# A gated Fourier and feed-forward mix on one core: five more couples of its big products at a second Strassen level

## The chip, the cores and the metric

The kernel runs on one core of a Trainium2 chip. The metric is the device time of one execution in microseconds (us); lower is better. TensorE (PE) multiplies, with PEld loading its weights; VectorE (DVE), ScalarE (ACT) and GpSimd (POOL) work on tiles; SyncE (SP) issues most loads.

## The reference, cut to what matters

```python
x = A_x                                            # 2048 x 1024
g = sigmoid((x * gate_w).sum(-1, keepdims=True))
a_ = einsum("bsd,ed->bse", x, dft_hid_re)          # 1024 x 1024 matrices
b_ = einsum("bsd,ed->bse", x, dft_hid_im)
a = einsum("ts,bse->bte", dft_seq_re, a_) - einsum("ts,bse->bte", dft_seq_im, b_)   # 2048 x 2048 matrices
h = relu(x @ w1 + b1) ** 2                         # w1: 1024 x 3584
b = h @ w2 + b2                                    # w2: 3584 x 1024
out = g * a + (1 - g) * b
```

All is float32.

## The kernel before, in words

**Stages.** The work is a list of *steps* in five stages, made in this order: `x_stage` (x times the hidden-dimension matrices, result `ab`), `c_stage` (the sequence stage: `ab` with the 2048 x 2048 matrices, result times g, stored as `gy`), `h_stage(0)` and `h_stage(1)` (the hidden layer, result `h`), and `o_stage` (the output stage: `w2` with `h`, plus bias, times 1 - g, plus `gy`, to `out`). Results between the stages go through DRAM. The list has 425 steps.

**A step** (`Group.run`, L297 to L315) multiplies a stationary operand of up to four column tiles (`rows`) and two contraction tiles with a moving operand of 512 columns. Each float32 operand is split in two: `hi` (a rounded copy, ScalarE, L220) and `lo` (the remainder, VectorE, L230); an operand of half width keeps both in one tile, `both`. Three matmuls (hi hi, hi lo, lo hi, L306) take the place of one, so that a step of four rows is 4 x 2 x 3 = 24 matmuls, one of two rows 12. Sums land in PSUM; the accumulator has four pairs of banks.

**Strassen, first level.** Every stage's product is cut in 2 x 2 blocks and computed as seven products instead of eight (Winograd's form, `seven`, L366), in the order 1, 2, 5, 6, 3, 7, 4. Their factors are blocks or sums of blocks: `SUMS_L` (S1 to S4) and `SUMS_R` (T1 to T4), which VectorE makes at L172 from tiles loaded by SP (L152). Results are put together as products end: `one` and `u` hold partial blocks, c11, c12, c21, c22 the final ones.

**Second level.** In the tall stages (`tall`, L412, for the sequence and the output stage) the contraction has 8 and 7 steps of two tiles (`ksteps`). A product goes either through `direct` (L445; its ksteps x 2 column blocks as steps of 24 matmuls) or through `twice` (L459). `twice` takes the first 2k contraction steps of a product as k *couples*, and computes each couple by seven smaller products of 12 matmuls each; the contraction steps that are left (`rest`) are done plainly. How many couples a product has stands in `TWICE_C` and `TWICE_O` (L20), product number to k. Before, the sequence stage has {2: 4, 3: 3, 4: 2} and the output stage {2: 3, 3: 3}.

The small products 1, 6, 7 and 5 of all couples come first; VectorE puts their results together (`one`, `six`, `seven_`, `five`, L477 to L527; adds at L438, L491, L493, L516, L519) with the partial result `old` that the product adds to, if there is one. Then 2, 4 and 3 are computed onto the blocks so made: `Group.prepare` (L279) has ScalarE copy a block back into PSUM (L293, `ps<-...`). The plain `rest` goes onto the same blocks, as steps of 12 matmuls.

**What sets the order.** One loop (L909 to L966) walks through the steps and puts down every instruction in program order, which each engine follows. For each step it loads tiles up to 12 steps ahead (`LOADS`) as SBUF has room (55 slots of 512 KB), issues POOL's stores, lets finished blocks go through `final` a few steps late (`LATER`), prepares the next step's PSUM, and puts sums, `hi` and `lo` ahead of their use: those due within three (`SUMS`) or two (`RESTS`) steps in any case, others up to nine steps ahead (`SPREAD`) if its own clocks for PE and VectorE say there is time. VectorE's queue thus holds sums, remainders and the putting together of results, in one fixed order.

In the first-level product 6 (L456) the T4 sums that product 4's couples need (`early`) are made while T2 is at hand, and stored to DRAM for product 4; the other T4 sums are made in product 4 from a stored T2.

**The end.** The last product's last block is finished row by row: `last` (L813 to L825) has VectorE add bias, multiply and add `gy` for one row of 512 columns at a time, and stores each at once (SP and ACT queues). Other blocks of `out` go through `final` (L827) and a store by POOL (L936).

Of the kernel before, what the change touches and what calls it, by code (L numbers as in the profile page):

```python
# [16 lines left out]
NF = F // P  # L17
SLOTS, KEEP, RAWS = 55, 5, 4
WIDE, TALL_C, TALL_O = ((1, 2, 5, 6, 3, 7, 4),) * 3
TWICE_X, TWICE_C, TWICE_O = (1, 2, 5, 3, 4), {2: 4, 3: 3, 4: 2}, {2: 3, 3: 3}  # L20
LATER = 3
WARM = 44
FAR_TALL, FAR_WIDE = ("T2",), ()
TWICE_H = (1, 2, 5, 3, 4), (2, 5, 3, 4)
# [17 lines left out]
def gated_mix_kernel(ctx: ExitStack, tc: tile.TileContext, x4, xn, w4, ct, w1a, w1b, w2, b1, b2, gw, out):  # L42
# [276 lines left out]
    def step(st, mv, group):  # L319
        st.uses += 1  # L320
        mv.uses += 1
        steps.append((st, mv, group, []))
        needs = 0
        count[group] = count.get(group, 0) + 1
        if count[group] % group.k == 0:
            needs += group.done[count[group] // group.k - 1][1]
        wanted.append(needs)
# [81 lines left out]
                    ends[e] = len(steps)  # L409
        return ends  # L410

    def tall(left, right, ksteps, order, second, target, final, last=None):  # L412

# [3 lines left out]
        left = {q: Sums(lambda i, j, q=q: left_(i, j, q), SUMS_L, far=FAR_TALL) for left_ in (left,) for q in range(ksteps)}  # L419
# [38 lines left out]

        def twice(p, old, new, ends, drop, sign):  # L459

            l, r = FACTORS[p]
            k = second[p]
            rest = range(2 * k, ksteps)
            more = len(rest)
            tmp = {key: Near("u") for key in ((0, 0),)}

# [67 lines left out]
            for q in range(k):  # L534
                for p2 in (1, 6, 7, 5):
                    l_, r_ = FACTORS[p2]
                    step(l2[q].operand(l_, 256), r2[q].operand(r_), groups[p2])

            def to(m, c):
                key = block(m, c)  # L540
                if last and p == order[-1] and (m, c) == (1, 1):
                    return Group(2, more, (lambda _, ps, row: last(new[key], ps, row), 0, [new[key]]),
                                 onto=[new[key]], by_row=True)
                return Group(2, k * ((m, c) != (1, 1)) + more, (lambda _, ps: put(new, key, ps, ends), 0, [new[key]]),
                             onto=[new[key]])

            groups = {2: to(0, 0), 3: to(0, 1), 4: to(1, 0), None: to(1, 1)}
            for q in range(k):
                again = Sums(lambda j, c, q=q: right[2 * q + j, c].of(r), SUMS_R, True)
                again.made.update({key: r2[q].of(key) for key in ("T1", "T2")})  # L550
                for p2 in (2, 4, 3):
                    l_, r_ = FACTORS[p2]
                    step(l2[q].operand(l_, 256), again.operand(r_), groups[p2])
            own = []
            for q in rest:
                st = left[q].operand(l)
# [223 lines left out]
    def c_stage():  # L780
        rows = [Row(n, False) for n in range(2)]
        to = {}

        def target(i, n, k):
            near = Near("y")
            to[near] = i, n, *k
            return near

        def final(dst, ps):
            i, n, c, rp = to[dst]  # L790
            nc.vector.tensor_tensor(dst.slot, dst.slot if ps is None else ps, rows[n].of(c).broadcast_to([P, 2, 512]),
                                    op=ALU.mult)
            vec(VEC[0] + VEC[1])
            rows[n].used()
            stores.append((gy[i, n, c, rp], dst, 0, 2))

        at = len(steps)
        tall(lambda i, j, q: ab[j, q, i], lambda j, n, q, c: ct[n, c, j, q], 8, TALL_C, TWICE_C, target, final)
        return at, rows


    def o_stage():
# [37 lines left out]

        fetched = {}
        at = len(steps)
        ends = tall(lambda i, j, q: w2[i, j, q], lambda j, n, q, c: h_far[j, q, 2 * n + c], 7, TALL_O, TWICE_O, target, final, last)
        return at, rows, fetched, ends

    def want(k, *items):
# [157 lines left out]
```

## Time and profile before

| | |
|---|---|
| median of 3 runs | 1891.29 us (1889.42 to 1892.37) |
| the profiled execution's own time | 1888.96 us |
| its span, first to last instruction | 1886.9 us |
| mean granted TensorE clock | 0.999 |
| instructions in the span | 21962 |
| ScalarE busy | 1001.3 us (53%) |
| GpSimd busy | 86.8 us (5%) |

A row of the groups or of the timeline names the line, the engine, the operation, the tiles (out<-in) and their shape, then a count, busy time and mean duration; in the timeline the first two numbers are start and length in us, and the brackets give idle time of the engine before it and what ended it. A matmul's record lasts longer than the distance to the next, since matmuls are pipelined. "Waits" rows give who waited for whom: us in total, how often, the longest.

### The profile page before, as it was taken

What the parts mean: (1) busy time and instruction counts of PE and PEld (TensorE: products, weight loads), DVE (VectorE), ACT (ScalarE), POOL (GpSimd) and SP (SyncE); (2) the same over time, 40 slices, a digit from 0 to 9 for tenths busy, and PEclk for the clock granted to TensorE, in tenths of its full rate; (3) what the DMA queues carried; (4) which work ended last, traced back from release to release, by engine and by line L of the source; (5) the groups of instructions that cost most, each with busy time, mean ns of one, the idle gap of its engine ahead of it and who ended that gap; (6) DMA issues with size and microseconds to landing.
All of it is one profiled execution on the core that took longest, in us unless ns stands there. A gap on an engine that the chain in (4) does not pass through costs nothing.

```text
span 1886.9 us, 21962 instructions
## 1 busy us (share of the span) xinstructions
PE 1876.6 (99%) x8288; PEld 1551.3 (82%) x8288; DVE 1610.3 (85%) x1543; ACT 1001.3 (53%) x1123; POOL 86.8 (5%) x161
## 2 busy tenths in 40 slices
PE   9999999999999999999999999999999999999998
PEld 7888888888888888888888888888888888888887
DVE  8997898599777998798896997989976997789882
ACT  6474564363343554455484797767954434264440
POOL 0000110000010000000000000000100001000000
PEclk9999999999999999999999999999999999999999
DMA  5732989339786489383551865628872887629971
GB/s 223 247 121 86 348 288 412 129 117 375 261 312 256 151 322 383 139 312 112 170 198 56 325 228 195 228 84 299 293 259 97 317 336 265 218 103 370 409 300 45
DMA packets 128425, 442.93 MB, mean 235 GB/s; under 512 B 14128, under 2 KB 23616, under 8 KB 128320
## 3 DMA queue, kind: packets, MB, share of 16 engines
q1 hardware_dynamic: 106416, 363.26, 53.0%
q0 software_dynamic: 21472, 77.61, 10.3%
q8 instruction: 65, 1.06, 0.2%
q10 hardware_dynamic: 432, 0.66, 0.1%
q14 instruction: 40, 0.33, 0.1%
HBM read 362.83 MB, written 78.65 MB: 234 GB/s over the span
## 4 chain that ended last, share of the span: by engine, by line
PE 97%; DVE 2%; ACT 0%; DMA 0%; issue 0%; SPq 0%; DVEq 0%; ACTq 0%
PE ps L306 97%; DVE lo L230 1%; DVE h L603 0%; DVE sum L172 0%; DMA raw<-in_w 0%; DVE o L818 0%; ACT u L596 0%; ACT hi L220 0%; DVE o L820 0%; DVE raw L172 0%; SPq L152 0%; DVEq L172 0%; DVEq L230 0%; ACTq L596 0%
## 5 line engine op out<-in xcount | busy, mean ns | idle before, releaser
L306 PE MATMUL ps<-hi 128*128 128x512 f32 x2328 | 905.7, 390 | 4.0 <-ACT hi L220 3.6
L306 PE MATMUL ps<-lo,hi 128*128 128x512 f32 x2328 | 905.3, 389 | 0.0
L306 PE MATMUL ps<-hi,lo 128*128 128x512 f32 x2328 | 904.2, 389 | 0.1
L220 ACT ACTIVATE hi<-raw 128x1024 fp32r<-128x1024 f32 (+2 forms) x413 | 420.6, 1037 | 399.0 <-DVE raw L172 274.1
L230 DVE TENSOR_TENSOR lo<-raw,hi 128x1024 fp32r<-128x1024 f32 (+2 forms) x413 | 484.5, 1199 | 57.5 <-ACT hi L220 31.3
L306 PEld LDWEIGHTS ps<-hi 128*128 128x128 f32 x2328 | 437.2, 188 | 95.9 <-ACT hi L220 4.2
L306 PEld LDWEIGHTS ps<-hi,lo 128*128 128x128 f32 x2328 | 437.1, 188 | 92.0 <-DVE lo L230 1.0
L306 PEld LDWEIGHTS ps<-lo,hi 128*128 128x128 f32 x2328 | 437.3, 188 | 91.0 <-DVE lo L230 0.4
L172 DVE TENSOR_TENSOR raw<-raw 128x1024 f32<-128x1024 f32 (+1 forms) x276 | 326.4, 1207 | 56.4 <-DMA raw<-in_ct 19.4
L220 ACT ACTIVATE hi<-sum 128x1024 fp32r<-128x1024 f32 (+1 forms) x172 | 176.1, 1036 | 184.8 <-DVE sum L172 151.2
L306 PE MATMUL ps<-hi,both 128*128 128x512 f32 x840 | 259.8, 389 | 0.0
L230 DVE TENSOR_TENSOR lo<-sum,hi 128x1024 fp32r<-128x1024 f32 (+1 forms) x172 | 203.3, 1198 | 32.9 <-PE ps L306 16.6
L306 PEld LDWEIGHTS ps<-hi,both 128*128 128x128 f32 x840 | 157.7, 188 | 33.8 <-ACT ps L293 0.7
L306 PE MATMUL ps<-lo,both 128*128 128x512 f32 x420 | 163.5, 389 | 0.0
L172 DVE TENSOR_TENSOR sum<-raw 128x1024 f32<-128x1024 f32 (+1 forms) x116 | 121.9, 1066 | 35.4 <-PE ps L306 28.1
L172 DVE TENSOR_TENSOR sum<-raw,sum 128x1024 f32<-128x1024 f32 (+2 forms) x87 | 96.8, 1119 | 12.0 <-PE ps L306 11.7
L603 DVE TENSOR_TENSOR h<-h,ps 128x1024 f32<-128x1024 f32 x92 | 98.2, 1086 | 9.6 <-ACT u L596 7.1
L596 ACT ACTIVATE u<-ps 128x1024 f32<-128x1024 f32 x76 | 71.9, 950 | 62.0 <-PE ps L306 54.3
L306 PEld LDWEIGHTS ps<-lo,both 128*128 128x128 f32 x420 | 78.8, 188 | 16.1
L293 ACT ACTIVATE ps<-u 128x1024 f32<-128x1024 f32 (+1 forms) x74 | 70.0, 953 | 22.2 <-DVE o L831 12.0
L700 ACT ACTIVATE h<-h,b1c 128x512 f32<-128x512 f32 x112 | 74.3, 712 | 6.3 <-DVE h L603 6.0
L220 ACT ACTIVATE both<-sum 128x512 fp32r<-128x512 f32 x60 | 37.1, 625 | 52.7 <-DVE sum L172 33.4
(61 smaller groups left out, 650.5 us busy)
## 6 DMA issues: line engine op xcount, KB each, us to landing
raw<-in_ct SPq DMA_DIRECT2D x151, 512.0 KB, 6.2
raw<-h SPq DMA_DIRECT2D x132, 512.0 KB, 7.3
raw<-in_x SPq DMA_DIRECT2D x107, 512.0 KB, 5.3
raw<-in_w SPq DMA_DIRECT2D x98, 512.0 KB, 6.3
raw<-ab SPq DMA_DIRECT2D x72, 512.0 KB, 6.8
h<-h POOLq DMA_DIRECT2D x48, 512.0 KB, 5.7
raw<-in_w1a SPq DMA_DIRECT2D x36, 512.0 KB, 5.0
ab<-ab POOLq DMA_DIRECT2D x32, 512.0 KB, 6.7
```

Of the source, the lines that this page charges most:

```text
L172: nc.vector.tensor_tensor(self.slot[:, k, c], src[0][:, k, c], src[1][:, k, c], op=self.op)
L220: nc.scalar.activation(self.hi[:, k, c], self.block.slot[:, k, c], AF.Copy)
L230: nc.vector.tensor_tensor(self.lo[:, k, c], self.block.slot[:, k, c], self.hi[:, k, c].bitcast(F32), op=SUB)
L293: nc.scalar.activation(t[:, :n, :], b.slot[:, at:at + n, :], AF.Copy, scale=self.sign)
L306: nc.tensor.matmul(self.ps[r // self.per][:, r % self.per, :], a[:, kk, r * P:(r + 1) * P], b[:, kk, :], start=self.at == 1 and kk + n == ...
L596: nc.scalar.activation(view(near.slot, k), view(ps, k), AF.Copy, scale=float(sign))
L603: nc.vector.tensor_tensor(view(near.slot, k), view((src or dst)[k].slot, k), view(ps, k), op=ADD if sign > 0 else SUB)
L700: nc.scalar.activation(dst.slot[:, k, :], (dst.slot if ps is None else ps)[:, k, :], AF.Relu, bias=b1c[:, tile0 + k:tile0 + k + 1])
```

## The change

`TWICE_C` gets three couples instead of two for product 4 of the sequence stage; `TWICE_O` gets two couples each for products 1 and 4 of the output stage. New are the lists `FIRST_C` and `FIRST_O`: for a product that has no partial result to add to, or that stands in the list (product 2 of the sequence stage, where nothing is left over; products 2 and 4 of the output stage), the `rest` comes first, as steps of 24 matmuls, onto the old partial result, and leaves its own partial blocks by `put`; the couples then go onto those. In the last product, where no `rest` is left at the end, the small product 4 comes last, and its block is the one that is finished row by row. With four contraction steps of product 4 in couples, the output stage also makes eight of its T4 sums early, in product 6.

```diff
-TWICE_X, TWICE_C, TWICE_O = (1, 2, 5, 3, 4), {2: 4, 3: 3, 4: 2}, {2: 3, 3: 3}
+TWICE_X, TWICE_C, TWICE_O = (1, 2, 5, 3, 4), {2: 4, 3: 3, 4: 3}, {1: 2, 2: 3, 3: 3, 4: 2}
+FIRST_C, FIRST_O = (2,), (2, 4)
...
         def twice(p, old, new, ends, drop, sign):
             l, r = FACTORS[p]
             k = second[p]
             rest = range(2 * k, ksteps)
+            if rest and (not old or p in first):
+                some = [Group(4, len(rest), (lambda rp, ps, c=c: put(new, (c, rp), ps, sign=sign), 2 * (old is not new),
+                                             [new[c, rp] for rp in range(2)]),
+                              onto=old and [old[c, rp] for rp in range(2)], spend=drop) for c in range(2)]
+                sts = {q: left[q].operand(l) for q in rest}
+                for q in rest:
+                    for c in range(2):
+                        step(sts[q], right[q, c].operand(r), some[c])
+                old, rest, drop = new, (), False
             more = len(rest)
...
-                if last and p == order[-1] and (m, c) == (1, 1):
-                    return Group(2, more, (lambda _, ps, row: last(new[key], ps, row), 0, [new[key]]),
+                if last and p == order[-1] and (m, c) == ((1, 1) if more else (1, 0)):
+                    return Group(2, more or k, (lambda _, ps, row: last(new[key], ps, row), 0, [new[key]]),
                                  onto=[new[key]], by_row=True)
...
+            own = []
             for q in range(k):
...
                 for p2 in (2, 4, 3):
                     l_, r_ = FACTORS[p2]
-                    step(l2[q].operand(l_, 256), again.operand(r_), groups[p2])
+                    own.append((l2[q].operand(l_, 256), again.operand(r_), groups[p2]))
+            if last and p == order[-1] and not more:
+                own.sort(key=lambda e: e[2] is groups[4])
+            for e in own:
+                step(*e)
...
-        tall(lambda i, j, q: ab[j, q, i], lambda j, n, q, c: ct[n, c, j, q], 8, TALL_C, TWICE_C, target, final)
+        tall(lambda i, j, q: ab[j, q, i], lambda j, n, q, c: ct[n, c, j, q], 8, TALL_C, TWICE_C, FIRST_C, target, final)
...
-        ends = tall(lambda i, j, q: w2[i, j, q], lambda j, n, q, c: h_far[j, q, 2 * n + c], 7, TALL_O, TWICE_O, target, final, last)
+        ends = tall(lambda i, j, q: w2[i, j, q], lambda j, n, q, c: h_far[j, q, 2 * n + c], 7, TALL_O, TWICE_O, FIRST_O, target, final, last)
```

The list of steps grows from 425 to 434.

More of the change, by code (lines that the diff above doesn't have):

```diff
@@ L410, in seven, with tall @@
         return ends
[L412 removed]
+    def tall(left, right, ksteps, order, second, first, target, final, last=None):
         left = {q: Sums(lambda i, j, q=q: left_(i, j, q), SUMS_L, far=FAR_TALL) for left_ in (left,) for q in range(ksteps)}
```

## The prediction

> **What bounds the kernel now.** I read the page first (span, engines, the chain that ended last), then the chain in order of time, then a table of windows by product of the output stage.
>
> ```profile
> span 1886.9 us, 21962 instructions
> PE 1876.6 (99%) x8288; PEld 1551.3 (82%) x8288; DVE 1610.3 (85%) x1543; ACT 1001.3 (53%) x1123; POOL 86.8 (5%) x161
> PE 97%; DVE 2%; ACT 0%; DMA 0%; issue 0%; SPq 0%; DVEq 0%; ACTq 0%
> ...
> 14.91 1257.50 PE ps L306 x5538
> ...
> 1300.11 577.56 PE ps L306 x2546
> ```
>
> The first two rows say that TensorE matmuls fill 99% of the span; the chain says the same by a stronger measure, 97% of what ended last is matmuls at L306. The two long pieces are unbroken matmul streams: 1257.50 us / 5538 = 0.227 us and 577.56 / 2546 = 0.227 us for each matmul. So the time is the number of matmuls times 0.227 us plus a short head and tail, as long as operands come in time. Whether they do is VectorE's matter (85% busy), and here the average hides the stages. The columns below are PE, PEld, DVE, ACT and POOL busy us; the seven stretches are products 1, 2, 5, 6, 3, 7, 4 of the output stage.
>
> ```profile
> 1364.60:1440.80 76.20, 76.20 (x338) 63.08 (x337) 49.27 (x51) 35.01 (x43) 2.15 (x4) 1.00 0.58 211
> 1440.80:1508.80 68.00, 68.00 (x301) 56.20 (x300) 63.85 (x67) 34.72 (x40) 0.98 (x2) 1.00 0.66 247
> 1508.80:1585.00 76.20, 76.20 (x338) 63.07 (x337) 62.70 (x56) 31.86 (x31) 5.13 (x9) 1.00 0.79 293
> 1585.00:1661.20 76.20, 76.20 (x338) 63.10 (x337) 56.02 (x54) 26.19 (x30) 4.23 (x8) 1.00 0.61 217
> 1661.20:1729.20 68.00, 68.00 (x301) 56.16 (x300) 66.85 (x72) 38.99 (x45) 1.08 (x2) 1.00 0.65 244
> 1729.20:1805.40 76.20, 76.20 (x338) 63.08 (x337) 64.38 (x59) 33.52 (x33) 1.81 (x3) 1.00 0.94 364
> 1805.40:1881.70 76.30, 76.30 (x337) 62.81 (x335) 44.00 (x45) 16.76 (x18) 4.28 (x6) 1.00 0.44 168
> ```
>
> Products 1 and 4 are plain and use VectorE for 49.27 and 44.00 of some 76 us; products 2 and 3, already at the second level, use it for 63.85 and 66.85 of 68.00, with TensorE still full. The change spends the room in the first and the last row.
>
> **TensorE: what is removed.** A couple (two contraction tiles) done plainly takes 4 steps of 24 matmuls, at the second level 7 steps of 12: 84 for 96. Product 4 of the sequence stage goes from two couples to three, products 1 and 4 of the output stage from none to two each: five couples, 60 matmuls. The built programs agree: 8244 matmuls at L306 before, 8184 after; so that the change doesn't do what it says is out. 60 x 0.227 = **-13.6 us**, all on the path, 2.7 in the sequence stage and 5.45 in each of the two products.
>
> The Trainium skill, page "TensorE: Matmul & The Clock Gate", section "Back-to-back issue gap", gives about 131 ns for a sustained matmul of 512 columns. By that the removal would be worth 7.9 us (an estimate); the chain's 0.227 us speaks against it here, so the sum stays with the rows.
>
> **VectorE: what is added.** Pitches, from instructions that stand back to back:
>
> ```profile
> 1435.54 1.23 DVE L230 TENSOR_TENSOR lo<-sum,hi 128x1024 fp32r<-128x1024 f32 x1 [1.43 <-PE ps L306]
> 1436.68 1.22 DVE L230 TENSOR_TENSOR lo<-raw,hi 128x1024 fp32r<-128x1024 f32 x1
> ...
> 1448.91 0.69 DVE L172 TENSOR_TENSOR sum<-raw 128x512 f32<-128x512 f32 x1 [0.31 <-PE ps L306]
> 1449.52 0.68 DVE L230 TENSOR_TENSOR both<-sum,both 128x512 fp32r<-128x512 f32 x1
> ```
>
> The 1024-wide instruction lasts 1.23 us, but the next begins 1436.68 - 1435.54 = 1.14 us after it; the 512-wide one takes 0.61. Each couple adds 4 half-wide left sums, 4 full right sums, 7 half-wide remainders ("both") and, 7 full ones for 6, one full remainder: 11 x 0.61 + 5 x 1.14 = 12.4 us, 62 us for five. Products 1 and 4 of the output stage also put their four partial blocks together (one copy, then 1 + 2 + 2 + 3 adds) in place of plain copies: 8 x 1.14 = 9.1 us each. Together about **80 us of VectorE**: 34 in each of the two output products and 12 in the sequence stage, of which 4 sums (4.6 us) move forward into product 6. The engine's share goes from 1610 / 1887 to some 1690 / 1877 = 90%. ScalarE gets 61 instructions more at 53% busy, and SP one load more; neither was a bound.
>
> **Is it hidden? The margin, counted down VectorE's queue.** The tight place is the start of the output stage, where product 1 used to build the lead that product 2 eats.
>
> ```profile
> 1358.72 2.36 DVE L230 TENSOR_TENSOR lo<-raw,hi 128x1024 fp32r<-128x1024 f32 x2
> ...
> 1387.14 0.70 DVE L230 TENSOR_TENSOR both<-raw,both 128x512 fp32r<-128x512 f32 x1
> ...
> 1440.78 0.39 PE L306 MATMUL ps<-hi,both 128*128 128x512 f32 x1
> ...
> 1493.52 2.35 DVE L230 TENSOR_TENSOR lo<-raw,hi 128x1024 fp32r<-128x1024 f32 x2
> ...
> 1508.84 0.39 PE L306 MATMUL ps<-hi 128*128 128x512 f32 x1
> ```
>
> The first remainder of the stage is done at 1361.1 (1358.72 + 2.36) and its step starts at 1364.6, where the first window begins: a lead of 3.5 us. The first remainder for product 2 is done at 1387.8, 52.9 us before its step at 1440.78. The first of product 5 is done at 1495.9 (it is the second of the pair, 1493.52 + 2.35), 13 us before its step at 1508.84. In the queue of the built program, from the first of these to the last, stand 72 full and 35 half instructions before, 72 x 1.14 + 35 x 0.61 = 103 us, done in 134.8: 31 us were waits, taken out of a lead that could afford them. After, the same stretch holds 91 full and 61 half ones, 141 us, against PE's 144.2 - 5.4 = 138.8 us and the 3.5 us of lead. Without any wait the lead at product 5 is 138.8 + 3.5 - 141 = about 1 us. So this stage has hardly anything over, and every wait that VectorE keeps comes off 1 us. What it waited for:
>
> ```profile
> DVE sum L172 <- PE ps L306: 14.7, 6, 3.9
> DVE g L767 <- DMA g<-g_far: 6.3, 1, 6.3
> ...
> DVE raw L172 <- DMA raw<-h: 7.7, 5, 3.6
> ```
>
> The first (in product 1) is waiting for a buffer that TensorE still reads: it goes when VectorE is no longer 50 us ahead. The second, the gate's row, can stay; in the built program its load now stands some five VectorE instructions ahead of its use. The third (in product 5 and behind) hits when there is little lead. So lateness there lies between 0 and 6.3 - 1 = 5 us, or 7.7 more if all these waits stay; when TensorE is late by that once, all later due times shift. I take **+1.3**, near the lower end, because the large wait is the kind that vanishes. Product 4 at the end has 74 us of queue for 71 of PE, but starts with the 21 us of lead that product 7 built; I cost it at nothing, and without that lead it would cost 3.
>
> In the sequence stage the thinnest lead is in product 3:
>
> ```profile
> 667.44 1.23 DVE L230 TENSOR_TENSOR lo<-raw,hi 128x1024 fp32r<-128x1024 f32 x1
> ...
> 669.31 0.84 PE L306 MATMUL ps<-hi,both 128*128 128x512 f32 x3
> ```
>
> The remainder ends at 668.67, its step begins with the second of the three matmuls, at 669.5: 0.9 us. The 4.6 us that move into product 6 mostly meet waits there; bounds 0 and 4.6, I take **+0.5**. The third couple of product 4 itself is paid in the lead of the hidden-layer stage that follows.
>
> **New hand-overs.** A second-level product ends by loading its own partial blocks back into PSUM, just after VectorE has put them together. Such a late load shows once:
>
> ```profile
> 1297.85 0.39 PE L306 MATMUL ps<-hi,lo 128*128 128x512 f32 x1
> 1298.56 1.02 PE L306 MATMUL ps<-hi 128*128 128x512 f32 x2 [0.33 <-ACT ps L293]
> ...
> 1300.11 0.50 PE L306 MATMUL ps<-hi,lo 128*128 128x512 f32 x1
> 1300.44 0.39 PE L306 MATMUL ps<-hi 128*128 128x512 f32 x1
> ```
>
> An idle time of 0.33 us cost more than itself: 6 matmuls from 1297.85 to 1300.44 took 2.59 us for 1.36, so 1.23 us. The change adds three such hand-overs (two blocks in product 1, one in product 4), so 0 to 3.7; I take **+2.0**, as VectorE is loaded in both.
>
> **The tail.**
>
> ```profile
> 1881.35 0.39 PE L306 MATMUL ps<-hi,lo 128*128 128x512 f32 x1
> ...
> 1883.36 0.34 ACTq L821 DMA_DIRECT2D out<-o  x1
> ...
> out<-o POOLq DMA_DIRECT2D x14, 512.0 KB, 6.8
> ```
>
> The last block is still written row by row behind the last matmul (2 us from 1881.35 to the issue at 1883.36). New is a 512 KB store by POOL whose block ends two steps (5.4 us) before TensorE does; with about 3 us of VectorE and 6.8 to land it comes some 5 us after the last matmul, where the last small stores land now. Bounds 0 and 2; I take **+0.4**.
>
> **The sum.** -13.6 + 1.3 + 0.5 + 2.0 + 0.4 = -9.4 us. The profiled execution took 1888.96 us (span 1886.9), so 1879.6; the median of the three runs is 2.3 us above it at 1891.29, so **1881.9**.
>
> **Rivals.** (a) *The saving is eaten in products 1 and 2 of the output stage:* VectorE keeps the gate row's wait and the loads' (6.3 + 7.7 - 1 = 13 us). Then -13.6 + 13 + 2.9 gives about +2: 1893.6, no change. For it: 141 us of queue for 142 us of time. Against it: those DMA waits were met at a lead of over 10 us, where the planner is in no hurry. Within it lies the clock. After the head's gap the matmuls run at about half pace:
>
> ```profile
> 14.91 0.80 PE L306 MATMUL ps<-hi 128*128 128x512 f32 x1 [2.91 <-ACT hi L220]
> 15.50 0.63 PE L306 MATMUL ps<-lo,hi 128*128 128x512 f32 x1
> 15.93 0.63 PE L306 MATMUL ps<-hi 128*128 128x512 f32 x1
> ```
>
> 0.43 us apart instead of 0.227, for some 3 us; a stall of 3 us thus costs up to 1.5 us on top. The same page of the Trainium skill, section "Why this matters for your kernels", warns of idle gaps of over about 3 us for this reason; the row agrees. (b) *Slower:* VectorE can't run without gaps for 141 us, and works at its mean share of 85%. Then the stretch takes 141 / 0.853 = 165 us, 23 over the 142 there are, and the end is -13.6 + 23 + 2.9 = +12: 1903.6. It decides from a share below 0.9 (141 / 0.9 = 157, 15 late). Against it stand products 2 and 3, at 94 and 98% of their windows. (c) *Nothing is late:* -13.6, 1877.7.
>
> **How the numbers follow.** About 0.2% (3.8 us) is what a measurement of this kernel can tell. Forecast 0.62 (some us of lateness), (c) 0.18, (a) 0.10, (b) 0.10. Faster: the first two, 0.80; of (a) most is no change, 0.09; slower 0.11. Range: from 1877 (nothing late, and the runs' scatter) to 1890 (lateness at 5, hand-overs at 3.7, the rest at their upper ends: -13.6 + 5 + 3.7 + 1.5 + 2 = -1.4).
>
> **What would show it.** Right: matmuls 8184, DVE near 1690 us busy, chain again 97% PE, new idle of PE only as a handful of gaps under 1 us before L294 loads and operands in products 1, 2 and the start of 5. The step "VectorE's waits vanish" is wrong if the wait for buffers stays above 10 us in the new product 1 or if PE idles by several us before a "lo" or "both" at products 2 and 5. The step "product 4 is covered" is wrong if PE waits in the last 40 us. The forecast is wrong as a whole if PE's chain breaks into pieces with DVE between.

## The result, and the profile after

The changed kernel takes 1883.33 us (median of 7 runs, 1879.46 to 1886.93) against 1891.11 us for the kernel before in the same comparison (1889.42 to 1892.37): a ratio of 0.9959, 95% interval 0.9949 to 0.9969, or -7.8 us. Forecast were 1881.9 and -9.4. The profiled execution took 1881.64 us, 7.32 less than the one before.

The page of the changed kernel, first the span, the busy times and the shares of the chain. All line numbers of helpers are one higher than before (matmuls L307, loads of PSUM L294, sums L173, `hi` L221, `lo` and `both` L231).

```profile
span 1879.6 us, 22035 instructions
...
PE 1866.2 (99%) x8228; PEld 1541.3 (82%) x8228; DVE 1686.0 (90%) x1638; ACT 1044.1 (56%) x1184; POOL 87.6 (5%) x162
...
PE 94%; DVE 4%; DMA 1%; ACT 1%; issue 0%; SPq 0%; DVEq 0%; ACTq 0%
```

PE has 60 instructions less and VectorE is at 1686.0 us, as worked out (1690). But the chain is 94% PE, not 97%: it breaks now. The chain in order of time (start, length, engine and line) shows where:

```profile
16.56 642.75 PE ps L307 x2828
...
673.24 511.10 PE ps L307 x2252
...
1210.36 63.14 PE ps L307 x277
...
1301.20 108.03 PE ps L307 x476
...
1424.66 254.77 PE ps L307 x1122
...
1692.81 1.15 DVE o L505
...
1694.04 1.04 ACT ps L294
1695.12 178.03 PE ps L307 x784
```

Before, there were two unbroken streams with a seam at 1298; now there are new seams at 660 to 673 (product 3 of the sequence stage), at 1210 (product 2 in the second half of the hidden layer), at 1424 (product 1 of the output stage) and at 1694 (product 3 of the output stage). What ended last in them is mostly VectorE, up from 2 to 4% of the chain. Within the streams the distance is still 642.75 / 2828 = 0.227 us.

The table of windows of the output stage, products 1, 2, 5, 6, 3, 7, 4 (PE, PEld, DVE, ACT, POOL busy):

```profile
1365.70:1437.10 71.40, 71.13 (x313) 58.45 (x313) 70.49 (x77) 47.60 (x61) 2.15 (x4) 1.00 0.61 215
1437.10:1505.20 68.10, 68.10 (x302) 56.25 (x302) 67.87 (x76) 41.16 (x49) 1.22 (x2) 1.00 0.64 226
1505.20:1581.30 76.10, 76.10 (x337) 63.08 (x336) 70.50 (x63) 32.90 (x32) 3.83 (x7) 1.00 0.89 340
1581.30:1657.50 76.20, 76.20 (x338) 63.10 (x337) 59.69 (x57) 27.84 (x31) 5.34 (x10) 1.00 0.71 272
1657.50:1727.40 69.90, 68.26 (x301) 56.26 (x300) 69.19 (x76) 38.05 (x45) 1.06 (x2) 1.00 0.61 228
1727.40:1803.60 76.20, 76.20 (x337) 63.12 (x337) 64.30 (x60) 33.57 (x33) 1.83 (x3) 1.00 0.95 366
1803.60:1874.50 70.90, 70.88 (x313) 58.43 (x311) 69.71 (x77) 34.81 (x42) 5.00 (x7) 1.00 0.34 122
```

Products 1 and 4 are down from 76.20 and 76.30 us to 71.40 and 70.90. VectorE works 70.49 of 71.40 and 67.87 of 68.10 us in products 1 and 2, nearly without a gap, and TensorE stands idle for 0.27 us there. The one stretch with a larger hole is product 3, which the change doesn't edit: 69.90 us for 68.26 of matmuls. It was 68.00 before.

To see the cost at each place I took all distances between neighbouring matmul starts at L307 from the trace and added up what lies above 0.227 us, for distances over 0.245. These sums (us) hold the idle time and the slower matmuls behind it:

| place | before | changed | forecast of the difference |
|---|---|---|---|
| head of the kernel | 5.10 | 5.56 | none |
| sequence stage, product 3 | 0.07 | 2.33 | 0.5 |
| sequence stage, product 4 (new hand-over) | 0.16 | 0.23 | part of 2.0 |
| hidden layer, second half, product 2 | 0 | 0.69 | none |
| hidden layer, second half, product 3 | 1.23 | 1.24 | none |
| output stage, product 1 (two new hand-overs) | 0 | 0.63 | rest of 2.0 |
| output stage, lateness in products 1, 2, 5 | 0 | 0 | 1.3 |
| output stage, product 3 | 0.06 | 1.92 | none |
| **together** | **6.62** | **12.60** | 3.8, and 0.4 for the tail |

So 6.0 us of the 13.6 saved are lost again, and some 0.4 in distances too small for the table: the last matmul starts at 1874.10 instead of 1881.35, 7.25 us earlier, and -13.6 + 6.0 + 0.4 = -7.2.

The two large places are hand-overs: a block that VectorE has just put together is copied back into PSUM by ScalarE (L294), and TensorE waits for it. The waits of PE over the whole trace, us in total, times, longest:

```profile
PE ps L307 <- ACT ps L294: 3.4, 5, 1.6
...
PE ps L307 <- DVE lo L231: 0.6, 1, 0.6
PE ps L307 <- DVE h L620: 0.2, 1, 0.2
```

(Before, one wait for such a copy: the 0.33 us that the prediction shows.) PE's timeline in product 3 of the sequence stage, with the idle time before each matmul in brackets:

```profile
662.81 0.51 PE L307 MATMUL ps<-hi,both 128*128 128x512 f32 x1 [0.56 <-ACT ps L294]
663.94 0.50 PE L307 MATMUL ps<-hi,both 128*128 128x512 f32 x1 [0.63 <-ACT ps L294]
```

And product 3 of the output stage, first VectorE and ScalarE, then PE:

```profile
1692.72 1.22 DVE L505 TENSOR_TENSOR o<-o,u 128x1024 f32<-128x1024 f32 x1
...
1694.04 1.03 ACT L294 ACTIVATE ps<-o 128x1024 f32<-128x1024 f32 x1 [2.59 <-DVE o L505]
```

```profile
1693.08 0.40 PE L307 MATMUL ps<-lo,both 128*128 128x512 f32 x1
1695.12 0.50 PE L307 MATMUL ps<-hi,both 128*128 128x512 f32 x1 [1.64 <-ACT ps L294]
```

The add at L505 ends at 1693.94, the copy starts 0.1 us later and ends at 1695.07, and the matmul starts right behind it. TensorE was through with the step before at some 1693.5 (1693.08 + 0.40). The hand-over is old: product 3 was at the second level before, too, and there the copy came in time. VectorE reaches it later now.

### The profile page after: what moved, and what is told of

It reads as the page before. It is cut to its first block, busy times and chain, and to the rows that moved or that the text cites. A ratio compares the mean times of both kernels' runs of the same rounds, so it can differ in the third digit from the quotient of the medians.

```text
span 1879.6 us, 22035 instructions
## 1 busy us (share of the span) xinstructions
PE 1866.2 (99%) x8228; PEld 1541.3 (82%) x8228; DVE 1686.0 (90%) x1638; ACT 1044.1 (56%) x1184; POOL 87.6 (5%) x162
## 4 chain that ended last, share of the span: by engine, by line
PE 94%; DVE 4%; DMA 1%; ACT 1%; issue 0%; SPq 0%; DVEq 0%; ACTq 0%
PE ps L307 94%; DVE lo L231 1%; DVE h L620 1%; DVE sum L173 1%; DMA raw<-in_x 0%; DVE u L503 0%; DMA raw<-in_w1b 0%; DMA g<-g_far 0%; DVE both L231 0%; DVE raw L173 0%; ACT ps L294 0%; ACT h L717 0%; ACT hi L221 0%; DVE o L505 0%; SPq L153 0%
## 5 line engine op out<-in xcount | busy, mean ns | idle before, releaser
L307 PE MATMUL ps<-hi 128*128 128x512 f32 x2168 | 844.3, 390 | 3.3 <-ACT hi L221 2.7
L307 PE MATMUL ps<-lo,hi 128*128 128x512 f32 x2168 | 844.1, 390 | 0.0
L307 PE MATMUL ps<-hi,lo 128*128 128x512 f32 x2168 | 843.3, 390 | 0.7 <-DVE lo L231 0.6
L221 ACT ACTIVATE hi<-raw 128x1024 fp32r<-128x1024 f32 (+2 forms) x398 | 406.8, 1037 | 370.6 <-DVE raw L173 245.7
L231 DVE TENSOR_TENSOR lo<-raw,hi 128x1024 fp32r<-128x1024 f32 (+2 forms) x398 | 468.3, 1197 | 45.5 <-ACT hi L221 28.4
L307 PEld LDWEIGHTS ps<-hi 128*128 128x128 f32 x2168 | 407.5, 188 | 89.7 <-ACT hi L221 3.5
L307 PEld LDWEIGHTS ps<-hi,lo 128*128 128x128 f32 x2168 | 407.6, 188 | 86.3 <-DVE lo L231 2.1
L307 PEld LDWEIGHTS ps<-lo,hi 128*128 128x128 f32 x2168 | 407.4, 188 | 84.4 <-DVE lo L231 0.4
L173 DVE TENSOR_TENSOR raw<-raw 128x1024 f32<-128x1024 f32 (+1 forms) x276 | 325.6, 1206 | 57.4 <-DMA raw<-in_ct 13.6
L307 PE MATMUL ps<-hi,both 128*128 128x512 f32 x1120 | 347.9, 390 | 3.1 <-ACT ps L294 3.1
L221 ACT ACTIVATE hi<-sum 128x1024 fp32r<-128x1024 f32 (+1 forms) x192 | 196.8, 1038 | 184.5 <-DVE sum L173 170.1
L231 DVE TENSOR_TENSOR lo<-sum,hi 128x1024 fp32r<-128x1024 f32 (+1 forms) x192 | 228.0, 1200 | 31.5 <-PE ps L307 18.2
L307 PEld LDWEIGHTS ps<-hi,both 128*128 128x128 f32 x1120 | 210.3, 188 | 49.4 <-ACT ps L294 5.5
L307 PE MATMUL ps<-lo,both 128*128 128x512 f32 x560 | 218.3, 390 | 0.1
L173 DVE TENSOR_TENSOR sum<-raw 128x1024 f32<-128x1024 f32 (+2 forms) x136 | 140.3, 1048 | 13.0 <-PE ps L307 9.3
L173 DVE TENSOR_TENSOR sum<-raw,sum 128x1024 f32<-128x1024 f32 (+2 forms) x102 | 112.4, 1107 | 13.3 <-PE ps L307 10.3
L307 PEld LDWEIGHTS ps<-lo,both 128*128 128x128 f32 x560 | 105.2, 188 | 22.0 <-DVE lo L231 0.6
L294 ACT ACTIVATE ps<-u 128x1024 f32<-128x1024 f32 x79 | 76.9, 980 | 20.7 <-DVE o L848 7.1
L221 ACT ACTIVATE both<-sum 128x512 fp32r<-128x512 f32 x80 | 49.6, 625 | 58.6 <-DVE sum L173 43.6
```

What stands on the lines that cost most here:

```text
L173: nc.vector.tensor_tensor(self.slot[:, k, c], src[0][:, k, c], src[1][:, k, c], op=self.op)
L221: nc.scalar.activation(self.hi[:, k, c], self.block.slot[:, k, c], AF.Copy)
L231: nc.vector.tensor_tensor(self.lo[:, k, c], self.block.slot[:, k, c], self.hi[:, k, c].bitcast(F32), op=SUB)
L294: nc.scalar.activation(t[:, :n, :], b.slot[:, at:at + n, :], AF.Copy, scale=self.sign)
L307: nc.tensor.matmul(self.ps[r // self.per][:, r % self.per, :], a[:, kk, r * P:(r + 1) * P], b[:, kk, :], start=self.at == 1 and kk + n == ...
```

## The experiments

All were timed in five rounds beside the kernel before on the same chip, whose median there was between 1889.84 and 1890.49 us. The letters for the theories are those of the expectations. Theory A is what the two traces suggested: the loss is made of hand-overs and late operands at the places in the table, because VectorE and its loads have no lead left there; each place has its own price, and what is undone at one place comes back. Its rivals are set against it run by run.

**Only the output stage changed** (product 4 of the sequence stage keeps two couples):

```diff
-TWICE_X, TWICE_C, TWICE_O = (1, 2, 5, 3, 4), {2: 4, 3: 3, 4: 3}, {1: 2, 2: 3, 3: 3, 4: 2}
+TWICE_X, TWICE_C, TWICE_O = (1, 2, 5, 3, 4), {2: 4, 3: 3, 4: 2}, {1: 2, 2: 3, 3: 3, 4: 2}
```

> Products 1 and 4 of the output stage at the second level as in the change, product 4 of the sequence stage left at two couples. Theory A (each removed matmul is worth 0.227 us, and TensorE loses time only at a few named places, each tied to the VectorE work that the change puts just ahead of it): 48 matmuls fewer, -10.9 us; the 2.3 us lost in product 3 of the sequence stage go back to 0.1, those in the output stage (0.6 in product 1, 1.9 in product 3) stay: -8.2, some 1882.9, the same as the whole change. Theory B (the loss is spread: every couple nets the same, -7.8 / 5 = -1.6 us): -6.2, some 1884.9.

1886.88 us (1883.22 to 1888.33, 11 runs), ratio 0.998 [0.9971, 0.9989]; -3.5 us. The loss in product 3 of the sequence stage is gone (0.07 us), as A says, but the time is not the 1882.9 that A gave: product 3 of the output stage loses 6.15 us in this trace instead of 1.92. How one place can cost 2 us in one run and 6 in another is taken up at the repeated kernel below.

**Only the sequence stage changed:**

```diff
-... {2: 4, 3: 3, 4: 3}, {1: 2, 2: 3, 3: 3, 4: 2}
-FIRST_C, FIRST_O = (2,), (2, 4)
+... {2: 4, 3: 3, 4: 3}, {2: 3, 3: 3}
+FIRST_C, FIRST_O = (2,), ()
```

> Only the third couple in product 4 of the sequence stage; the output stage as before. Theory A: 12 matmuls fewer, -2.7 us, but four T4 sums more in product 6 of that stage, and product 3 behind it loses 2.3 us where it lost 0.1, and some 0.3 elsewhere: -0.2 us, no difference, and TensorE idle before product 3's late steps by some 2 us. Theory B: -1.6 us.

1890.27 us (1889.23 to 1893.04, 11 runs), ratio 1.0002 [0.9993, 1.0011]. The third couple removes 12 matmuls, 2.7 us, and brings nothing. PE's timeline in product 3 of that stage:

```profile
663.23 0.50 PE L307 MATMUL ps<-hi,both 128*128 128x512 f32 x1 [0.90 <-ACT ps L294]
664.36 0.50 PE L307 MATMUL ps<-hi,both 128*128 128x512 f32 x1 [0.63 <-ACT ps L294]
```

The same two hand-overs are late, and with a late operand at 673.65 the place loses 2.08 + 0.62 = 2.7 us: the whole saving. So this loss belongs to this couple and doesn't need the output stage. That refutes theory B.

**Only product 1, and only product 4, of the output stage:**

```diff
-... {2: 4, 3: 3, 4: 3}, {1: 2, 2: 3, 3: 3, 4: 2}
-FIRST_C, FIRST_O = (2,), (2, 4)
+... {2: 4, 3: 3, 4: 2}, {1: 2, 2: 3, 3: 3}
+FIRST_C, FIRST_O = (2,), (2,)
```

> Only product 1 of the output stage at the second level (and product 2's left-over step first). Theory A: 24 matmuls fewer, -5.45 us, 0.6 us lost at its own hand-over back into PSUM; no T4 sums move, so that the 1.9 us in product 3 of the output stage go: -4.8 us, some 1886.3. Theory B: -3.1 us.

```diff
-... {2: 4, 3: 3, 4: 3}, {1: 2, 2: 3, 3: 3, 4: 2}
-FIRST_C, FIRST_O = (2,), (2, 4)
+... {2: 4, 3: 3, 4: 2}, {2: 3, 3: 3, 4: 2}
+FIRST_C, FIRST_O = (2,), (4,)
```

> Only product 4 of the output stage at the second level. Theory A: -5.45 us, and the 1.9 us lost in product 3 of the output stage appear, since the eight T4 sums for product 4 are made in product 6 ahead of it: -3.5 us, some 1887.6. Theory B: -3.1 us. A third theory, C (the late hand-over in product 3 is the inheritance of a loaded product 1, not of the T4 sums): no loss in product 3, -5.4 us.

Product 1 alone: 1885.68 us (1884.03 to 1886.39, 9 runs), ratio 0.9973 [0.9964, 0.9983], -4.7 us where A gave -4.8. Product 4 alone: 1885.45 us (1884.27 to 1887.63, 11 runs), 0.9976 [0.9967, 0.9985], -4.9 us, between what A and C gave. Each has 5.45 us to save and keeps most of it. What each costs at the hand-over in product 3, which neither edits, is in the traces: 0.89 us lost with product 1 alone, 0.45 with product 4 alone, 0.06 with neither, and 1.92 to 6.15 with both. That is more than the sum. With product 1 alone A had expected no loss there at all, so the place doesn't hang on the T4 sums only. A reading of these four numbers, which no run tests by itself: product 1 uses up the lead that VectorE would bring from the start of the stage, and product 4 adds early sums and their loads to product 6, just ahead of product 3; each alone leaves a rest of lead, both leave none. Together the two gains would be 9.6, and the first run shows 3.5.

**No early sums for the third couple.** The T4 sums of the sequence stage's third couple are made in product 4 from a stored T2, not ahead in product 6:

```diff
-                if p == 6 and q < 2 * second.get(4, 0):
+                if p == 6 and q < min(4, 2 * second.get(4, 0)):
```

> The whole change, but the four T4 sums that the third couple needs in the sequence stage are made in product 4 and no longer early in product 6 (the first eight stay early; the output stage is as in the change). Theory A: the 2.3 us lost in product 3 of the sequence stage go back to 0.1, product 4 there pays up to 1 us for its four sums: -1.5 us against the change, some 1881.8. Rival E (product 3 is late because of its own place, not because of these sums): the loss of 2.3 us in product 3 stays, no gain.

1890.69 us (1887.32 to 1894.07, 11 runs), ratio 1.0005 [0.9996, 1.0014]: the whole gain is gone. A was right on the place, since product 3 of the sequence stage loses 0.07 us again; it was wrong on the price in product 4, where it gave 1 us at most and 6.5 were lost. ScalarE's and PE's timelines there, and VectorE's waits between 800 and 840 us:

```profile
833.46 1.03 ACT L294 ACTIVATE ps<-y 128x1024 f32<-128x1024 f32 x1 [4.88 <-DVE y L440]
```

```profile
834.54 0.50 PE L307 MATMUL ps<-hi,both 128*128 128x512 f32 x1 [4.15 <-ACT ps L294]
```

```profile
DVE raw L173 <- DMA raw<-copy: 3.8, 1, 3.8
```

VectorE waited 3.8 us for the stored T2, all that stood behind it in its queue was late, and so was the block (`y`) that the hand-over copies: TensorE stood for 4.15 us, after which the granted clock was 0.50 for 3.4 us (836 to 839 us). The early sums that cost 2.3 us in product 3 save more in product 4.

**A changed order of the small products.** Within a group of couples the small products 2, 4, 3 of a couple follow one another. Here the small product 2 of the next couple comes ahead of the 4 and the 3 of this one, so that the first couple's 4, the first onto its block, comes one step later:

```diff
+            own = sorted(own, key=lambda e: (own.index(e) - (2.5 if e[2] is groups[2] and own.index(e) else 0)))
             if last and p == order[-1] and not more:
                 own.sort(key=lambda e: e[2] is groups[4])
```

> The whole change, with one thing more: in each second-level product the small product 2 of the second couple stands before 4 and 3 of the first (2 2 4 3 2 4 3 ... instead of 2 4 3 2 4 3 ...), so that the two blocks that go back into PSUM last have one step of 12 matmuls (2.7 us) more of cover. Theory A (TensorE loses time where VectorE has just put a block together that must go back into PSUM; where the wait passes some 1.7 us the clock halves on top, which makes the scatter): the losses at the hand-overs go, 1.7 us in product 3 of the sequence stage, 0.2 in its product 4, 0.6 and 1.9 in products 1 and 3 of the output stage, and the scatter of the runs (7.5 us over 7) shrinks to some 3: about 1879, 4 us under the change itself. Theory D (VectorE's queue is late as a whole; a later hand-over only moves the wait to the next operand): the same time as the change within 1.5 us.

1879.63 us (1878.83 to 1885.98, 5 runs), ratio 0.995 [0.9937, 0.9963]; -10.7 us. Of the changed kernel's losses, the hand-overs in product 1 of the output stage and in product 4 of the sequence stage are gone, and product 3 of the sequence stage falls from 2.33 to 1.16 us. Product 3 of the output stage still loses 2.82 us: 1.9 at the hand-over, as late as in the changed kernel (1.68 us idle against 1.64), and 0.9 at a remainder 9 us behind it. D is refuted by the time, since it gave the changed kernel's within 1.5 us; of its mechanism this late remainder is left. The same kernel on another chip:

> The kernel with the changed order alone (2 2 4 3 ...) once more, beside the two, since its first five runs held one of 1886 among four of 1879 to 1880. Theory A: a median of 1879 to 1881, and in its trace a loss in product 3 of the output stage between 0.5 and 4 us, as the loads before it land. Rival D (the order only moves the wait): 1882 to 1885.

1880.81 us (1879.26 to 1881.83, 5 runs), 0.995 [0.9936, 0.9963]. In PE's timeline, product 3 of the output stage:

```profile
1694.12 0.50 PE L307 MATMUL ps<-hi,both 128*128 128x512 f32 x1 [0.32 <-ACT ps L294]
...
1703.40 0.50 PE L307 MATMUL ps<-lo,both 128*128 128x512 f32 x1 [0.59 <-DVE lo L231]
```

It loses 1.44 us, half by the hand-over and half by an operand. Product 3 of the sequence stage loses 2.16 here, so what the order saves there is not certain; the output stage's product 1 loses nothing in either trace.

**Both edits at once** (the changed order, and no early sums for the third couple):

```diff
-                if p == 6 and q < 2 * second.get(4, 0):
+                if p == 6 and q < min(4, 2 * second.get(4, 0)):
...
+            own = sorted(own, key=lambda e: (own.index(e) - (2.5 if e[2] is groups[2] and own.index(e) else 0)))
```

> Both edits of the two runs before this one together. Theory A: TensorE loses only what it lost before the change (6.6 us, of which 5 in the head) and some 1.5 us in product 4 of the sequence stage and about 1 in the output stage: -13.6 + 2.5, some 1879 to 1880 and a scatter of 3 us. Theory D: as the change, 1882 to 1883.

1886.1 us (1884.55 to 1888.61, 8 runs), 0.9978 [0.9968, 0.9989]. No loss is left in product 3 of the sequence stage, and 5.8 us are lost in its product 4: worse than the order alone by 6.5 us on the same chip, and slower than A (1879 to 1880) and D (1882 to 1883) gave. The early sums are worth their place.

**The changed kernel again**, with no edit, beside these on one chip:

> The change itself once more, unaltered, beside the three others and for a second trace. Theory A: its median within 2 us of 1883.3 with a scatter of several us, and the loss in product 3 of the output stage another than 1.9 us, since it depends on when VectorE's loads land in products 5 and 6; the rest of the losses the same to 0.3 us. If the scatter were the chip's, the kernel before would show it too in the same rounds.

1884.64 us (1881.48 to 1886.79, 6 runs), ratio 0.9971 [0.9959, 0.9982]. So the order is worth 5.0 us on this chip (1879.63 against 1884.64). The profiled execution took 1886.56 us, 4.9 more than the first profile of the same program, and the table of lost time has 17.8 us instead of 12.6. Of the 5.2 us, 3.8 lie in product 3 of the output stage, 5.69 against 1.92; 0.8 lie at 945 us, where the first trace lost nothing, so the other losses did not all stay the same to 0.3 us as A gave. PE's timeline of this run at that place:

```profile
1696.39 0.50 PE L307 MATMUL ps<-lo,both 128*128 128x512 f32 x1 [1.61 <-DVE lo L231]
1698.64 0.80 PE L307 MATMUL ps<-hi,both 128*128 128x512 f32 x1 [1.75 <-ACT ps L294]
1699.23 0.63 PE L307 MATMUL ps<-lo,both 128*128 128x512 f32 x1
```

Here a remainder is late as well, 2 us ahead of the hand-over, and behind both the matmuls take 0.80 and 0.63 us where 0.50 and 0.39 are usual. The table of windows around it (the seventh figure, ahead of the DMA share and GB/s, is the granted clock):

```profile
1698.00:1702.00 4.00, 3.36 (x8) 2.68 (x9) 4.00 (x5) 2.98 (x4) 0.00 (x0) 0.57 0.01 5
1702.00:1706.00 4.00, 4.00 (x18) 3.27 (x18) 4.00 (x5) 3.23 (x4) 0.00 (x0) 1.00 0.44 132
```

8 matmuls in 4 us against 18: the granted clock was 0.57 on the mean of these 4 us, and 0.50 from 1698.6 to 1702.0, for 3.4 us. The same window of the first profile of this kernel, after its single idle time of 1.64 us:

```profile
1694.50:1698.50 4.00, 3.38 (x15) 2.81 (x16) 4.00 (x5) 2.98 (x4) 0.00 (x0) 1.00 0.28 105
```

The clock stayed at 1.00. That is the step from 2 us to 6: a second idle time, 2.0 us between starts, and 1.9 us for matmuls at half the clock behind it. The run with only the output stage changed shows the same pair (1.30 and 1.75 us, 2.3 us apart), the clock at 0.50 for 6.8 us, and 6.15 us lost. What decides whether the clock falls is taken up at the end. The kernel before, whose idle times there are under 0.1 us, varied by 3 us on this chip (19 runs), the changed one by 5.

What VectorE waits for ahead of this place, from product 5 to the hand-over in product 3 (1505 to 1697 us), first in the changed kernel's first profile, then in this one:

```profile
DVE raw L173 <- DMA raw<-in_w: 10.6, 5, 5.9
...
DVE raw L173 <- DMA raw<-h: 7.9, 4, 6.1
```

```profile
DVE raw L173 <- DMA raw<-h: 13.0, 5, 6.7
DVE raw L173 <- DMA raw<-in_w: 9.0, 5, 6.3
```

18.5 and 22.0 us of waits for loads of `w2` (`in_w`) and of `h`, against 13.8 in the kernel before (8.1 for `h`, 5.7 for `in_w`). These loads come with sums, the early ones among them. They are only part of the difference: VectorE waits 4.7 us longer than before for them in the first profile, but it comes into product 5 with 1.9 us of lead instead of 13.

**More room for loads.** `RAWS` bounds how many slots the loaded tiles that VectorE hasn't taken up yet may hold; past it, a tile is loaded only when its use is at most three steps away. If the loads are what takes the lead, 6 instead of 4 should help:

```diff
-SLOTS, KEEP, RAWS = 55, 5, 4
+SLOTS, KEEP, RAWS = 55, 5, 6
```

> The whole change with up to six loaded tiles waiting for VectorE instead of four (RAWS = 6), so that loads are issued earlier. It tests what makes VectorE late in product 3 of the output stage. Theory A, as it stands after the runs so far (VectorE has no lead left there because it waited some 18 to 22 us for loads in products 5 and 6 of the output stage; what is lost at the hand-over in product 3, 1.9 us in one trace of the change and 5.7 in the other, follows those landings): these waits fall to under 8 us, the loss in product 3 to under 1 us, and the time to 1880 to 1881 with a smaller scatter. Rival F (VectorE's amount of work, not its waits): waits fall but the loss in product 3 stays at 2 us or more, the time within 1.5 us of the change.

1890.14 us (1885.04 to 1892.31, 11 runs), 0.9997 [0.9988, 1.0005]. In the output stage A has the direction, not the size: VectorE's waits for the two loads fall to 7.9 + 6.3 = 14.2 us where it gave under 8, and product 3 loses 1.16 where it gave under 1. The time is neither A's (1880 to 1881) nor F's (within 1.5 us of the changed kernel). For the constant holds for all stages, and at the border from the first to the second stage a new hole opens, in PE's timeline:

```profile
290.74 0.80 PE L307 MATMUL ps<-hi 128*128 128x512 f32 x1 [3.42 <-DVE ab L620]
```

7.8 us are lost around this border and 3.7 in product 3 of the sequence stage: more than was won.

**The order and the room for loads together:**

```diff
-SLOTS, KEEP, RAWS = 55, 5, 4
+SLOTS, KEEP, RAWS = 55, 5, 6
...
+            own = sorted(own, key=lambda e: (own.index(e) - (2.5 if e[2] is groups[2] and own.index(e) else 0)))
```

> The changed order of the small products (2 2 4 3 ...) and RAWS = 6 together. Theory A: the hand-overs lose nothing, and the operands behind them are not late either: -13.6 + 0.5 to 1, 1877.5 to 1878.5, the best of all. Rival F: as the changed order alone, 1879.5 or more.

1884.92 us (1882.65 to 1887.04, 6 runs), 0.9969 [0.9958, 0.9981]. Product 3 of the output stage loses 0.28 us, the border 6.9: the same picture.

**The order, and the room in the output stage alone:**

```diff
-            if o.need > i + SUMS and o.room() + sum(e.room() for e in items[summed:loaded]) > RAWS:
+            if o.need > i + SUMS and o.room() + sum(e.room() for e in items[summed:loaded]) > (6 if i >= at else RAWS):
...
+            own = sorted(own, key=lambda e: (own.index(e) - (2.5 if e[2] is groups[2] and own.index(e) else 0)))
```

> The changed order of the small products (2 2 4 3 ...), and up to six loaded tiles waiting for VectorE in the output stage alone (four in the stages before it, where six cost 5 to 8 us at the start of the sequence stage). Theory A: in product 3 of the output stage TensorE loses 0.3 us, as in the run with six everywhere, where the changed order alone lost 1.4 and 2.8; the rest as the changed order alone: 1 to 2.5 us under its 1879.6 and 1880.8, some 1878 to 1879, and TensorE's other losses unchanged. Rival F (VectorE's amount of work, not its waits for loads, decides there): 1880 to 1881, no gain over the changed order alone.

1880.38 us (1877.22 to 1882.78, 5 runs), 0.9952 [0.9938, 0.9966]. The profiled execution took 1877.22 us, the shortest of all. Its table of windows for product 3 of the output stage, and VectorE's waits ahead of it (1505 to 1697 us):

```profile
1654.90:1723.00 68.10, 68.10 (x302) 56.24 (x301) 68.05 (x73) 39.35 (x46) 0.72 (x1) 1.00 0.62 227
```

```profile
DVE raw L173 <- DMA raw<-in_w: 6.4, 4, 2.8
DVE raw L173 <- DMA raw<-h: 6.0, 3, 2.5
```

The waits are 12.4 us and TensorE is full: 0.04 us lost. So the hole in product 3 closes with all couples and all of VectorE's work in place, when loads may come earlier: the three traces with six slots lose 1.16, 0.28 and 0.04 us there, those with four 1.92 and 5.69, and 1.44 and 2.82 with the changed order. That speaks against F as the mechanism. It doesn't make the loads the whole cause: the kernel before waited 13.8 us for them and lost 0.06, with more lead. VectorE's waits of all kinds in this stretch hardly fell either (22.3 us in the changed kernel's first profile, 21.2 here, 5.0 of them for ScalarE's `both`); no single wait for a load is over 2.8 us now, where 6.1 was the longest.

The lost time in the whole trace is 8.3 us, 1.7 above the kernel before. But this is the trace of the fastest of the five runs; what the others lose isn't known. In the time the step can't be told from the order alone: 1880.38 against 1879.63 and 1880.81, with ranges that overlap. That is what F gave (1880 to 1881), not A (1878 to 1879). Both versions beat the kernel before. The order alone also beat the changed kernel where the two ran on one chip, by 5.0 us in the median, though one of its five runs took 1885.98; the last version didn't run beside it.

## Why the prediction was right, and where its terms were off

**The mechanism held.** The time is the number of matmuls times 0.227 us plus what comes late; 60 matmuls less were worth 13.6 us, and the sum's sign and size follow. Of the rivals, (b) is refuted by the windows: VectorE works 98.7 and 99.7% of products 1 and 2 (70.49 / 71.40 and 67.87 / 68.10), not its mean share. (c) is refuted by the seams in the chain.

**Its own signs.** Two came out against it. The chain is 94% PE and breaks into pieces with VectorE between, which the prediction had named as the sign that the forecast is wrong as a whole; and there are idle times of up to 1.64 us, not only gaps under 1 us. The time came out near the forecast all the same, because the share of VectorE in the chain is not idle time of TensorE: in the whole trace TensorE loses only 6.0 us more than before. The sign was too coarse, as the kernel before had such a break too (1272 to 1300 us).

**VectorE in products 1 and 2 (forecast 1.3 us).** Nothing was lost there. The count down VectorE's queue was right: waits that took 14.7 and 6.3 us before are all but gone. VectorE's waits in product 1 (1365 to 1441 us):

```profile
DVE lo L231 <- ACT hi L221: 0.5, 2, 0.3
DVE g L784 <- DMA g<-g_far: 0.4, 1, 0.4
```

And the lead at the first step of product 5, VectorE's row and PE's:

```profile
1502.05 1.22 DVE L231 TENSOR_TENSOR lo<-raw,hi 128x1024 fp32r<-128x1024 f32 x1
...
1505.17 0.39 PE L307 MATMUL ps<-hi 128*128 128x512 f32 x1
```

The remainder is done at 1503.27 and its step starts at 1505.17: a lead of 1.9 us where 1 was worked out.

**New hand-overs (forecast 2.0 us).** The three cost 0.7: 0.63 in product 1 of the output stage and 0.07 in product 4 of the sequence stage. The term was too large, because its price was misread. The 1.23 us at 1298 before are not what one idle time of 0.33 us costs. Two copies came late there, one behind the other (the second of the two matmuls at 1298.56 starts 0.52 us after the first, behind the second copy), and then a remainder, as the chain before shows:

```profile
1297.95 2.11 DVE lo L230 x2
1300.06 0.04 issue
1300.11 577.56 PE ps L306 x2546
```

A single late copy costs less: idle times of 0.27 us (product 1) and 1.64 us (product 3) of the output stage cost 0.55 and 1.92, some 0.28 us more than the idle time itself. What was also overlooked is that an *old* hand-over becomes late where the change takes VectorE's lead. This step failed: hand-overs were counted by how many are new, not by how many stand where the lead is now thin.

**Product 3 of the output stage (not in the sum).** Priced at nothing, it costs 1.9 us in the first trace and 5.7 in the second. It is rival (a)'s mechanism, waits for loads that stay, in a mild form and later in the stage than it said: the 1.9 us of lead at product 5 had to last, and VectorE waited 18.5 us for loads until product 3. Before, it had 13 us of lead there and waited 13.8. The prediction's sentence that "all later due times shift" once TensorE is late didn't cover the case that TensorE is not late and VectorE is.

**Sequence stage (forecast 0.5 us).** It cost 2.26 in the first trace and all of the 2.7 us saved when alone. The step that failed is that the 4.6 us of sums moved into product 6 "mostly meet waits there". Without those sums product 3 loses 0.07 us. The upper bound named, 4.6, held. It is missing from the range, though: the sum for its upper end (-13.6 + 5 + 3.7 + 1.5 + 2) doesn't hold it. With 4.6 in place of the 1.5 it comes to 1.7 us above the kernel before, some 1893, instead of 1.4 below it.

The prediction also let the third couple itself be paid in the lead of the hidden layer, at nothing. Product 2 of that layer's second half loses 0.69 us now. It lost 0.37 to 0.73 in every trace with the third couple where `RAWS` was 4 in this stage, at most 0.08 in the two where it was 6, and nothing in the four traces without this couple. So it goes with the couple; how the lateness gets there isn't shown.

**Product 4 and the tail.** Product 4 of the output stage lost nothing, as costed. The tail cost 0 instead of 0.4. The last matmul, the store of 512 KB by POOL and the last small store's issue:

```profile
1874.10 0.39 PE L307 MATMUL ps<-hi,both 128*128 128x512 f32 x1
```

```profile
1872.64 0.72 POOL L953 DMA_DIRECT2D out<-o  x1 [1.87 <-DVE o L851]
...
1876.13 0.35 ACTq L838 DMA_DIRECT2D out<-o  x1
```

From the last matmul to the end of the span it is 5.5 us before and after.

**Sum.** Forecast losses were 1.3 + 0.5 + 2.0 + 0.4 = 4.2 us; measured were 6.0 in the table and 0.4 beside it. 0.46 of the 6.0 lie in the head, which the change doesn't touch (5.08 to 6.50 us over the traces). The total was near by luck: terms that were too large (hand-overs, products 1 and 2) stood beside terms that were too small or at nothing. In the repeated measurement the same kernel gained 5.6 us (1884.64 against 1890.28), farther from the 9.4 that were forecast; the direction held there too.

**Open.** Why the runs of the last version still scatter by 5 us, with its trace nearly free of holes; why one of the five runs of the changed order took 1885.98; and why more room for loads holds up `ab` at the border between the first two stages.

## What to carry to other kernels

When an edit fills an engine that was ahead, go on past the edited stretch and look for the next place where its result is needed at once: a step that costs nothing today may be held up by lead that comes from the edited part, and two edits that each leave a little lead can together leave none. Work moved forward ("made early") is paid where it lands, through the loads it brings as much as through its own time, but taking it back may cost more where it was needed. Before taking work out of a full engine's way, try the order of the steps: one small product moved ahead was worth 5.0 us here, nearly as much as two of the five couples.

## What was not expected of the hardware

Short idle times of TensorE can cost more than their length when they come close together. Two of 1.61 and 1.75 us within 2.3 us were followed by 3.4 us at a granted clock of 0.50, and the place lost 5.69 us, while one of 1.64 us alone left the clock at 1.00. The Trainium skill, page "TensorE: Matmul & The Clock Gate", section "Why this matters for your kernels", warns of idle gaps of over about 3 us. Single gaps of 4.15, 3.42 and 3.03 us (no early sums; `RAWS` = 6; the order and `RAWS` = 6) were followed by a clock of 0.50 for 3.4 us, as the page says. In the pair no single gap was that long and the clock fell too, so the row decides: in these traces two gaps close together can do what the page says of one long one.

Not every pair does it. One 9 us apart (1.68 and 0.60 us, in the first run of the changed order) left the clock at 1.00, and so did one of 2.19 and 0.73 us, 1.5 us apart, in the run with `RAWS` = 6. That also refutes the 1.7 us at which the expectation for the changed order let the clock halve. The clock records of the fourteen traces show what these cases have in common. Between the head and the last matmul, the clock changes only at whole multiples of 3.413 us from one another (in the second profile it fell 1679.36 us, 492 of them, after it had gone up). It fell five times, each time at the end of a stretch of this length in which no more than five matmuls had started, and never after one with six or more; at full pace there are 15. In the run with only the output stage changed it stayed at 0.50 behind a second stretch with five. So it matters how little TensorE does within one such stretch, and with that where in it the idle times fall.

A wait of TensorE costs a little more than the idle time that the profile shows. Behind the late starts at 1424.66 and 1695.12 (first profile of the changed kernel) the next matmul followed 0.34 us later instead of 0.227; and a matmul's record lasts 0.39 us where the next starts after 0.227, so that the idle time shown begins 0.16 us late. Together that is the 0.28 us named above.
